# Layer two's search with its bounds made earlier and its probes in halves; three low parts of the first weights on GpSimd, loads held until the first rows land

## The chip, the cores and the metric

The program runs on one core of one Trainium2 chip. The metric is the device time of one execution in microseconds. Engines are named as the profile names them: PE is TensorE (PEld its weight loads), DVE is VectorE, ACT is ScalarE, POOL is GpSimd, SP is SyncE, which issues the plain transfers.

## The reference

Attention, then two mixture-of-experts layers over 1792 tokens of 768 numbers, 8 experts of 768 x 1024 x 768, all in float32. The change is about layer two, where every expert takes exactly 224 tokens and the pairs of token and expert are served in order of their logit.

```python
def _moe2_ref(x, w_gate, w1, w2):
    N, D = x.shape
    E = w_gate.shape[1]
    cap = N // E
    logits = x @ w_gate
    order = np.argsort(-logits.flatten())
    assigned = -np.ones(N, dtype=np.int64)
    counts = np.zeros(E, dtype=np.int64)
    for idx in order:
        tok, e = (int(idx) // E, int(idx) % E)
        if assigned[tok] >= 0 or counts[e] >= cap:
            continue
        assigned[tok] = e
        counts[e] += 1
    out = np.zeros((N, D), dtype=np.float32)
    for e in range(E):
        mask = assigned == e
        h = np.maximum(x[mask] @ w1[e], 0.0)
        out[mask] = h @ w2[e]
    return out
```

## The kernel before

The program computes attention, layer one, and layer two one behind the other; each engine runs its instructions in program order, and there is no scheduler: the order is that of the code. Float32 products are made as three matmuls of a high and a low part each (`w1h xh`, `w1l xh`, `w1h xl`): ScalarE writes the high part as a rounded copy (line 857), VectorE subtracts it from the raw weights for the low part (line 858). A raw block of `w1` is 128 x 1024, 512 KB, and there are six of them, `k` = 0 to 5, for an expert.

Layer two does not sort. It takes the experts in the order in which they fill up, and for each one searches the threshold of the logit at which it is full. All tokens' logits stand in `L` (128 x 14 x 8), the best open one of each token in `t_mm` (128 x 14), its expert as a one-hot in `t_oh`. `search(p)` runs four rounds (`RN`). A round compares `t_mm` with 40 thresholds `thr` (`srch_89`) in one VectorE instruction of 128 x 560, the **probe** (`probe`, line 696, writes `t_g`); counts by 14 small matmuls (line 739); takes the largest excess over the capacity (line 740); makes a flag (`t_ok`, line 744); counts the flags by one matmul (line 752); and writes 40 new thresholds (line 755). After the last round it assigns the tokens (`t_asg`), counts them per expert (`tally`, `t_rab`, line 640 the sum over partitions), and `assign(p)` turns the assignment into a list of 224 row numbers (`idx`). The first bounds of the search come from the smallest and the largest entry of `L` (lines 519 to 533), with two transposes on TensorE (line 524) in the tail of layer one, whose last gate logits run between them (`tail0` to `tail3`, lines 240 to 257).

The search of the first expert to be served (p = 0) runs alone, from 579 to 595 in the trace; dummy groups of matmuls (`warm(n)`, lines 504, 541, 610) stand between its steps on TensorE. Then comes the **head** of layer two. SyncE issues the first weights, GpSimd the gather of the first rows (`gather`, 2 x 112 rows, line 865). The second expert's search is a generator that the head steps through with `go(1)`: its pieces stand in program order between dummy groups, the splitting of the weights (`split`), the transposes of the rows (`take`, which makes `xh` and `xl`, lines 892 to 896), and the first up matmuls (`up4`, line 914). `up4` does the first four of the eight column blocks, `k` by `k`, as the weights come; after it `up(4)` to `up(7)` (line 907) and the rest of the layer run as one stream of matmuls. The head of before in the code:

```python
        for k in range(KD):
            if k:
                go(1)
            if k + 2 < KD:
                split(0, k + 2)
            up4(k, 0, 2)
            if k in (2, 3):
                go(1)
            up4(k, 2, 4)
```

Eight raw buffers (`raw_90` to `raw_97`) take the weights. Before the loads of k = 3 to 7 GpSimd writes one element into each of these buffers (line 941), in its queue behind the gather's issue; so these loads go out when the gather is issued. A buffer is loaded again when both its high and its low part are made.

Of the kernel before, what the change touches and what calls it, by code (L numbers as in the profile page):

```python
# [127 lines left out]
def moe1(tc, w1, w2, wg, xs, y2, l2, ident, before, iob, cr, gt, g0, raw, early, iok, L, srch):  # L128
    nc = tc.nc
    with ExitStack() as c:  # L130
# [380 lines left out]
        d, hp, rh, oi, tk = xg[:, :128], xg[:, 128:256], xg[:, 256:256 + NB * E], xg[:, 512:512 + NB], xg[:, 640:641]  # L511
# [4 lines left out]
        V.scalar_tensor_tensor(hp, d, -float(NB), hp, op0=OP.is_gt, op1=OP.mult)  # L516
        V.tensor_tensor_reduce(d, d, hp, scale=-1.0, scalar=0.0, op0=OP.mult, op1=OP.add, accum_out=tk)
        V.tensor_scalar(oi, iok[:, :NB], tk, None, op0=OP.is_equal)
# [9 lines left out]
        V.tensor_reduce(gmn, pU[0][:, :128], axis=AX.X, op=OP.min)  # L528
        V.tensor_reduce(gmx, pU[0][:, 128:256], axis=AX.X, op=OP.max)
        V.tensor_sub(step, gmx, gmn)  # L530
        V.scalar_tensor_tensor(gmn, step, -0.25, gmn, op0=OP.mult, op1=OP.add)
        V.tensor_scalar(step, step, 1.5 / TH, None, op0=OP.mult)
        V.tensor_scalar(thr, iok[:, :TH], step, gmn, op0=OP.mult, op1=OP.add)
# [3 lines left out]
                     l2c[:, None, :].to_broadcast([128, NB, E]))  # L537
        nc.tensor.matmul(pU[1][:, :NB * E], hp, rh, start=True, stop=True)
# [5 lines left out]
def moe2(tc, w1, w2, y2, out, ident, before, ones, io8, iok, iob16, L, srch, raw, force):  # L544
# [7 lines left out]
    with ExitStack() as c:  # L552
# [141 lines left out]
        def probe():  # L694

            V.tensor_tensor(T["g"][:, :, :TH], T["mm"][:, :, None].to_broadcast([128, PT, TH]),
                            thr[:, None, :].to_broadcast([128, PT, TH]), op=OP.is_ge)

        def search(p):

            if p:
                best()
                V.tensor_tensor(T["oh"], T["lm"], T["m"][:, :, None].to_broadcast([128, PT, E]), op=OP.is_equal)
            else:
                V.tensor_reduce(T["mm"], L, axis=AX.X, op=OP.max)
                probe()
                V.tensor_tensor(T["oh"], L, T["mm"][:, :, None].to_broadcast([128, PT, E]), op=OP.is_equal)
            if p == E - 1:
# [23 lines left out]
            for r in range(RN):  # L732
# [24 lines left out]
                if r < RN - 1:  # L757
                    probe()
# [7 lines left out]
            if p == 0:  # L766
# [3 lines left out]
            V.scalar_tensor_tensor(apen, T["asg"], -BIG, apen, op0=OP.mult, op1=OP.add)  # L770
            V.scalar_tensor_tensor(T["full"], cap, 0.0, left, op0=OP.is_equal, op1=OP.mult)
            V.tensor_tensor_reduce(T["d"], t, T["capm"], scale=1.0, scalar=-3.0e38, op0=OP.subtract,
                                   op1=OP.max, accum_out=T["fl"][:, 0:1])

        def assign(p):

            V.tensor_reduce(T["em"], T["full"], axis=AX.X, op=OP.min)
            V.tensor_scalar(T["fl"][:, :2], T["fl"][:, :2], 0.0, None, op0=OP.not_equal)
            V.tensor_scalar(T["ei"], T["em"], 8.0, 7.0, op0=OP.add, op1=OP.min)
            EV[p] = nc.values_load(T["ei"][0:1, 0:1], engines=[SP], min_val=0, max_val=E - 1)  # L780
            V.tensor_scalar(T["mem"], own, T["em"], None, op0=OP.is_equal)
# [3 lines left out]
            V.scalar_tensor_tensor(bad, T["fl"][:, 0:1], T["fl"][:, 1:2], bad, op0=OP.mult, op1=OP.add)  # L785
            V.tensor_tensor_scan(T["cum"], T["mem"], T["mem"], 0.0, op0=OP.add, op1=OP.bypass)
            V.scalar_tensor_tensor(left, left, T["em"], left, op0=OP.not_equal, op1=OP.mult)
# [18 lines left out]
            for i in range(PT):  # L806
                nc.tensor.matmul(t[:16, :NA], T["b"][:, i], T["a"][:, i], start=(i == 0), stop=(i == PT - 1))
# [639 lines left out]
```

## Time and profile before

| | |
|---|---|
| median of 3 runs | 922.82 us (922.36 to 924.37) |
| the profiled execution | 920.12 us |
| its span on the core | 918.2 us |
| mean granted TensorE clock | 0.991 |
| PE busy | 867.1 us (94%) |
| DVE busy | 594.1 us (65%) |
| ACT busy | 475.1 us (52%) |
| POOL busy | 188.2 us (20%) |

The profiled execution is one further run; 1.9 us of it lie outside the span. Shares over the whole span average stages with different limits: the head of layer two is 13 us of it, and is to be read by itself.

### The profile page before, as it was taken

To read this page: it belongs to the slowest core of one execution; us is meant where nothing else is said; L and a number is where in the kernel's file an instruction comes from. 1 tells how busy PE (TensorE), PEld (TensorE's weight loads), DVE (VectorE), ACT (ScalarE), POOL (GpSimd) and SP (SyncE) were. 2 spreads that over 40 slices of the span, in tenths; PEclk is the share of its full clock that TensorE was granted. 3 is DMA by queue.
4 is the path that set the end of the run, shared out by engine and by line. 5 is a ranking of instruction groups with operands and counts; after the bars stand their busy time and mean duration, and the time that the engine had idled before them with its cause. 6 is when DMAs were issued, how large, how long until landed. Compare 5 with 4: busy or idle time off the path is not lost. (4 is left out here: it accounts for less than half of the span.)

```text
span 918.2 us, 18445 instructions
## 1 busy us (share of the span) xinstructions
PE 867.1 (94%) x6387; PEld 721.9 (79%) x6387; DVE 594.1 (65%) x1741; ACT 475.1 (52%) x1029; POOL 188.2 (20%) x249
## 2 busy tenths in 40 slices
PE   7999999987999998798999999889999999999997
PEld 5666666646788886676888888368989999999997
DVE  7779898877464526738611141798888798875641
ACT  8777777655454527648622242134545344545541
POOL 6644444041111111112111110101101011011001
PEclk9999999998999999999999999999999999999999
DMA  6553537148374616838721110177666575666810
GB/s 177 135 154 102 142 102 225 54 151 296 130 273 157 222 38 228 330 118 309 282 73 53 38 48 33 67 257 245 198 213 200 156 236 177 223 196 193 261 59 30
DMA packets 73921, 151.07 MB, mean 165 GB/s; under 512 B 30513, under 2 KB 38737, under 8 KB 73746
## 3 DMA queue, kind: packets, MB, share of 16 engines
q1 hardware_dynamic: 67602, 123.33, 41.2%
q0 software_dynamic: 6144, 25.72, 8.6%
q8 instruction: 72, 1.18, 0.5%
q14 instruction: 103, 0.84, 0.3%
HBM read 130.34 MB, written 18.67 MB: 162 GB/s over the span
## 5 line engine op out<-in xcount | busy, mean ns | idle before, releaser
L213 PE MATMUL pU<-w1h,xx 128*128 128x512 f32 x336 | 117.9, 408 | 3.7 <-ACT yr L236 1.6
L907 PE MATMUL w<-xh,w1h 128*128 128x224 f32 x360 | 102.2, 284 | 0.8 <-ACTq L995 0.8
L907 PE MATMUL w<-xh,w1l 128*128 128x224 f32 x360 | 99.0, 275 | 0.4 <-DVEq L995 0.4
L1163 ACT ACTIVATE p<-p,nm 112x112 f32<-112x112 f32 (+2 forms) x192 | 98.8, 517 | 0.7 <-DVE nm L1155 0.7
L907 PE MATMUL w<-xl,w1h 128*128 128x224 f32 x360 | 99.0, 275 | 0.0
L1155 DVE CUSTOM_DVE_ANT_0 p<-s,msk 112x112 f32<-112x112 f32 (+2 forms) x192 | 75.9, 444 | 22.5 <-PE s L1152 22.3
L930 PE MATMUL w<-w2h,hh 128*112 128x384 f32 x256 | 89.8, 351 | 0.0
L930 PE MATMUL w<-w2h,hl 128*112 128x384 f32 x256 | 86.5, 338 | 0.0
L930 PE MATMUL w<-w2l,hh 128*112 128x384 f32 x256 | 86.0, 336 | 0.0
L213 PEld LDWEIGHTS pU<-w1h,xx 128*128 128x128 f32 x336 | 62.8, 188 | 21.1 <-issue 2.6
L907 PEld LDWEIGHTS w<-xh,w1h 128*128 128x128 f32 x360 | 69.0, 192 | 1.5 <-ACTq L995 1.0
L907 PEld LDWEIGHTS w<-xh,w1l 128*128 128x128 f32 x360 | 69.1, 192 | 0.6 <-DVEq L995 0.6
L181 DVE TENSOR_TENSOR w2l<-raw,w2h 128x768 fp32r<-128x768 f32 x64 | 58.2, 956 | 17.1 <-ACT w2h L179 14.4
L907 PEld LDWEIGHTS w<-xl,w1h 128*128 128x128 f32 x360 | 69.1, 192 | 0.1
L231 PE MATMUL pY<-w2h,hh 128*128 128x384 f32 x224 | 60.6, 353 | 7.6 <-ACT w1h L179 4.7
L858 DVE TENSOR_TENSOR w2l<-raw,w2h 128x768 fp32r<-128x768 f32 x64 | 60.9, 951 | 8.6 <-ACT w2h L857 8.3
L213 PE MATMUL pU<-w1l,xx 128*128 128x512 f32 x168 | 65.8, 395 | 0.6 <-DVE w1l L460 0.6
L858 DVE TENSOR_TENSOR w1l<-raw,w1h 128x1024 fp32r<-128x1024 f32 x48 | 58.0, 1220 | 9.6 <-ACT w1h L857 9.3
L919 ACT ACTIVATE hh<-w 128x224 fp32r<-128x224 f32 x64 | 22.8, 357 | 79.0 <-PE w L907 56.1
L181 DVE TENSOR_TENSOR w1l<-raw,w1h 128x1024 fp32r<-128x1024 f32 x42 | 49.6, 1218 | 21.8 <-ACT w1h L179 21.8
L869 POOL DMA_INDIRECT out_dram<-yo,idx x15 | 15.2, 1011 | 218.2 <-ACT yo L933 181.8
L231 PE MATMUL pY<-w2l,hh 128*128 128x384 f32 x224 | 58.4, 342 | 0.0
(332 smaller groups left out, 2080.7 us busy)
## 6 DMA issues: line engine op xcount, KB each, us to landing
raw<-in_moe_w_dram SPq DMA_DIRECT2D x96, 512.0 KB
raw<-in_moe_w_dram SPq DMA_DIRECT2D x128, 384.0 KB
vt<-in_v_dram SPq DMA_DIRECT2D x48, 112.0 KB
qr<-in_q_dram SPq DMA_DIRECT2D x23, 224.0 KB
kr<-in_k_dram SPq DMA_DIRECT2D x23, 224.0 KB
xs<-xr SPq DMA_DIRECT2D x4, 1120.0 KB
xs<-xr SPq DMA_DIRECT2D x4, 238.0 KB
y<-yr SPq DMA_DIRECT2D x1, 384.0 KB
```

Of the source, the lines that this page charges most:

```text
L181: nc.vector.tensor_sub(l, r, h.bitcast(F32))
L213: nc.tensor.matmul(pU[half], a[:, k], w[:, k, cs], start=(m == 0), stop=(m == 17))
L231: nc.tensor.matmul(pY[g][:, :384], a[:, k], w[:, k, g * 384:(g + 1) * 384], start=(k == 0 and t == 0), stop=(k == KF - 1 and t == 2))
L858: V.tensor_sub(l, r, h.bitcast(F32))
L869: nc.gpsimd.indirect_dma_start(out=out, out_offset=bass.IndirectOffsetOnAxis(ap=idx[p % 3][:, g:g + 1], axis=0), in_=yo[:, g], in_offset=None)
L907: nc.tensor.matmul(u, w[:, k, fs], x[:, k], start=(k == 0 and n == 0), stop=(k == KD - 1 and n == 2))
L919: A.activation(hh[:, f], u, AF.Relu)
L930: nc.tensor.matmul(y, a[:, f, g * G2:(g + 1) * G2], w[:, f, hf * 384:(hf + 1) * 384], start=(f == 0 and n == 0), stop=(f == KF - 1 and n = ...
L1155: nc.vector.tensor_tensor_reduce(P[u, h][:, o:o + w], s[h][:, :w], msk[:, S - w:], scale=-0.125, scalar=3.0e38, op0=OP.add, op1=OP.min, ac ...
L1163: nc.scalar.activation(p, p, AF.Exp, bias=RS[u, "m"][:, h, i:i + 1], scale=-1.0, accum_out=RS[u][:, h, i:i + 1])
```

## The change

In the tail of layer one, the smallest and the largest entry of `L` are VectorE's first instructions, into a slice of their own (`mn2`), and the two transposes stand ahead of the gate's on TensorE; two groups of two dummy matmuls are left out, and `thr` is written later. In the first search the probe is issued as two instructions of 7 x 40, each a wait of its own for the matmuls, and `t_oh` is made ahead of it. The tally is merged with the comparison; the checks (`bad`, `t_fl`, `left`, `apen`) are put into `rest()`, which runs behind the running count (`cum`) of `assign`, or follow the matmuls of line 807. GpSimd issues a gather by a list of zeros before the search. The highs of k = 0 to 2 stand together ahead on ScalarE, followed by a copy of one element of the gathered rows into `raw[3]`, for which the loads of k = 3 and on wait on SyncE. The lows of k = 2, 3 and 5 are made by GpSimd. `up4` takes the products in two parts.

```diff
+        V.tensor_reduce(mn2[:, 0:1], L, axis=AX.XY, op=OP.min)
+        V.tensor_reduce(mn2[:, 1:2], L, axis=AX.XY, op=OP.max)
+        for n in range(2):
+            nc.tensor.transpose(pU[0][:, n * 128:n * 128 + 128], mn2[:, n:n + 1].to_broadcast([128, 128]), ident)
         V.tensor_copy(tk, sin)
...
-        V.tensor_reduce(d[:, 0:1], L, axis=AX.XY, op=OP.min)
-        V.tensor_reduce(d[:, 1:2], L, axis=AX.XY, op=OP.max)
-        tail1()
-        warm(2)
-        for n in range(2):
-            nc.tensor.transpose(pU[0][:, n * 128:n * 128 + 128], d[:, n:n + 1].to_broadcast([128, 128]), ident)
...
+        def probe(parts=1):
+
+            for i in range(parts):
+                s = slice(i * PT // parts, (i + 1) * PT // parts)
+                n = s.stop - s.start
+                V.tensor_tensor(T["g"][:, s, :TH], T["mm"][:, s, None].to_broadcast([128, n, TH]),
+                                thr[:, None, :].to_broadcast([128, n, TH]), op=OP.is_ge)
...
-                    probe()
+                    probe(1 if p else 2)
+            V.scalar_tensor_tensor(T["ao"], T["mm"][:, :, None].to_broadcast([128, PT, E]), thr[:, 0:1], T["oh"],
+                                   op0=OP.is_ge, op1=OP.mult)
+            with nc.allow_low_precision("small whole numbers"):
+                V.tensor_reduce(T["rab"], T["ao"].rearrange("p i e -> p e i"), axis=AX.X, op=OP.add)
             V.tensor_scalar(T["asg"], T["mm"], thr[:, 0:1], None, op0=OP.is_ge)
-            V.tensor_scalar(T["fl"][:, 2:3], T["fl"][:, 2:3], float(PT), None, op0=OP.not_equal)
-            tally()
-            V.tensor_add(bad, bad, T["fl"][:, 2:3])
             owned()
...
             V.tensor_tensor_scan(T["cum"], T["mem"], T["mem"], 0.0, op0=OP.add, op1=OP.bypass)
-            V.scalar_tensor_tensor(left, left, T["em"], left, op0=OP.not_equal, op1=OP.mult)
+            while late:
+                late.pop()()
...
             V.tensor_scalar(T["ev"], t[:16, :NA], float(N), None, op0=OP.min)
-            if p == 0:
-                warm(2)
...
-        def split(p, k):
+        def split(p, k, part=(True, True), on=V):
...
-            A.activation(h, r, AF.Copy)
-            V.tensor_sub(l, r, h.bitcast(F32))
+            if part[0]:
+                A.activation(h, r, AF.Copy)
+            if not part[1]:
+                return
+            on.tensor_sub(l, r, h.bitcast(F32))
...
-        def up4(k, f0, f1):
-            for f in range(f0, f1):
-                if k == 0:
+        def up4(k, part):
+            p = [(w1h, xh), (w1h, xl), (w1l, xh)]
+            if k < 2:
+                p = [p[0], p[2], p[1]]
+            for f in range(4):
+                if k == 0 and part == 0:
                     U[f] = wt()[:, :CAP]
-                for n, (w, x) in enumerate(((w1h, xh), (w1l, xh), (w1h, xl))):
-                    nc.tensor.matmul(U[f], w[:, k, f * 128:(f + 1) * 128], x[:, k], start=(k == 0 and n == 0),
-                                     stop=(k == KD - 1 and n == 2))
+                for w, x in p[2:] if part else p[:2]:
+                    nc.tensor.matmul(U[f], w[:, k, f * 128:(f + 1) * 128], x[:, k],
+                                     start=(k == 0 and (w, x) == (w1h, xh)), stop=(k == KD - 1 and part == 1))
...
         reset()
+        nc.gpsimd.memset(idx[0], 0)
+        gather(0, 1)
         finish(0)
         for k in range(3):
             load(0, k)
         gather(0)
+        for k in range(3):
+            split(0, k, (True, False))
+        A.activation(raw[3][:1, :1], xg[:1, 1, :1], AF.Copy)
         for k in range(3, NR):
-            nc.gpsimd.memset(raw[k][:1, :1], 0.0)
             load(0, k)
...
-        split(0, 0)
+        split(0, 0, (False, True))
...
-        split(0, 1)
+        split(0, 1, (False, True))
+        split(0, 2, (False, True), nc.gpsimd)
...
-            if k + 2 < KD:
-                split(0, k + 2)
-            up4(k, 0, 2)
+            if 3 <= k + 3 < KD:
+                split(0, k + 3, on=V if k == 1 else nc.gpsimd)
+            up4(k, 0)
             if k in (2, 3):
                 go(1)
-            up4(k, 2, 4)
+            up4(k, 1)
```

On GpSimd, the head of layer two stood like this before: the first expert's gather, five one-element writes, and the next expert's gather.

```order
L865 DMA xg<-y_103,idx_23704 112x768 x2
L941 MEMSET raw_93 1x1
L941 MEMSET raw_94 1x1
L941 MEMSET raw_95 1x1
L941 MEMSET raw_96 1x1
L941 MEMSET raw_97 1x1
L865 DMA xg<-y_103,idx_23705 112x768 x2
```

And now (the first of the three gathers is the one by zeros):

```order
L951 MEMSET idx_23702 112x2
L877 DMA xg<-y_103,idx_23702 112x768 x3
L870 TENSOR_TENSOR w1l<-raw_92,w1h 128x1024
L870 TENSOR_TENSOR w1l<-raw_93,w1h 128x1024
L870 TENSOR_TENSOR w1l<-raw_95,w1h 128x1024
L877 DMA xg<-y_103,idx_23703 112x768 x2
```

Three subtractions took the place of the five writes, each behind the high part of its block.

On VectorE, from the low parts of the rows (`xl`) to the probe of the second search's last round, before:

```order
L896 TENSOR_TENSOR xl<-w,xh 128x448 x3
L858 TENSOR_TENSOR w1l<-raw_92,w1h 128x1024
L740 ISA t_d,t_mx<-gp,t_capm 40x8
L740 ISA t_mx 40x1
L744 TENSOR_SCALAR t_ok<-t_mx 40x1
L748 ISA t_ao,t_fl<-t_oh 128x112
L748 ISA t_fl 128x1
L858 TENSOR_TENSOR w1l<-raw_93,w1h 128x1024
L755 SCALAR_TENSOR_TENSOR srch_89<-gp,steps,t_base 128x40
L696 TENSOR_TENSOR t_g<-t_mm,srch_89 128x14x40
```

And now:

```order
L908 TENSOR_TENSOR xl<-w,xh 128x448 x3
L743 ISA t_d,t_mx<-gp,t_capm 40x8
L743 ISA t_mx 40x1
L747 TENSOR_SCALAR t_ok<-t_mx 40x1
L751 ISA t_ao,t_fl<-t_oh 128x112
L751 ISA t_fl 128x1
L870 TENSOR_TENSOR w1l<-raw_94,w1h 128x1024
L758 SCALAR_TENSOR_TENSOR srch_89<-gp,steps,t_base 128x40
L697 TENSOR_TENSOR t_g<-t_mm,srch_89 128x14x40
```

One subtraction is left in this piece, that of k = 4; behind the probe another (`raw_94` before) and one later (`raw_95`) are gone too.

On TensorE, in the tail of layer one, from the branch on, before (`pU_3390` are the two transposes of the bounds, `pB` and `pA` the gate's):

```order
L444 UNCONDITIONAL_BRANCH
L240 MATMUL pB_3388<-ident,yr 128x128 x4
L240 MATMUL pB_3389<-ident,yr 128x128 x2
L504 LDWEIGHTS before
L504 MATMUL pU_3391<-iob,before 128x512
L504 LDWEIGHTS before
L504 MATMUL pU_3391<-iob,before 128x512
L524 MATMUL pU_3390<-ident,xg 128x128 x2
L250 MATMUL pA_3387<-hb,wg_101 32x128 x4
```

And now:

```order
L444 UNCONDITIONAL_BRANCH
L515 MATMUL pU_3390<-ident,xg 128x128 x2
L240 MATMUL pB_3388<-ident,yr 128x128 x4
L240 MATMUL pB_3389<-ident,yr 128x128 x2
L250 MATMUL pA_3387<-hb,wg_101 32x128 x4
```

The bounds' transposes moved from between the gate's two steps to ahead of both, and the dummy pair between them is gone.

## Rows read from the trace of the kernel before

**Rows 1.** Windows by stage: us, busy (instructions) by engine, clock, DMA share.

```profile
605.20:618.00 12.80, 10.86 (x104) 9.69 (x104) 12.01 (x46) 5.35 (x9) 0.00 (x0) 1.00 0.77 277
618.00:630.00 12.00, 12.00 (x107) 11.69 (x106) 10.56 (x23) 7.64 (x15) 2.51 (x6) 1.00 0.67 202
650.00:912.00 262.00, 258.93 (x2086) 246.65 (x2085) 187.33 (x533) 117.61 (x193) 27.61 (x27) 1.00 0.57 183
```

**Rows 2.** TensorE's waits from 605.2 to 625: total, times, longest us.

```profile
PE gp L739 <- DVE t_g L696: 0.6, 1, 0.6
...
PE gp L752 <- DVE t_ok L744: 0.4, 1, 0.4
```

**Rows 3.** Timeline where the search is set up: start, duration us.

```profile
575.73 0.60 ACT L241 ACTIVATE hb<-pB 128x512 f32<-128x512 f32 x1 [0.42 <-PE pB L240]
...
576.71 0.43 PE L250 MATMUL pA<-hb,wg 128*32 128x128 f32 x8
```

**Rows 4.** Timeline, a later round of the first search.

```profile
583.28 0.51 PE L739 MATMUL gp<-t_oh,t_g 128*40 128x8 bf16 x14 [0.16 <-DVE t_g L696]
```

**Rows 5.** Timeline, end of the first assignment on TensorE.

```profile
594.05 0.60 PE L610 MATMUL w<-iob,before 128*128 128x512 bf16 x2
...
594.59 0.21 PE L813 MATMUL gp<-t_ev,sel 16*112 16x15 f16 x1
```

**Rows 6.** Timeline of the head, first layer-two expert.

```profile
597.45 1.06 ACT L857 ACTIVATE w1h<-raw 128x1024 fp32r<-128x1024 f32 x1 [0.69 <-DMA raw<-in_moe_w_dram]
...
600.33 0.74 DVE L696 TENSOR_TENSOR t_g<-t_mm,srch 128x560 bf16<-128x560 f32 x1
...
601.40 1.22 DVE L858 TENSOR_TENSOR w1l<-raw,w1h 128x1024 fp32r<-128x1024 f32 x1
...
605.26 0.37 PE L914 MATMUL w<-xh,w1h 128*128 128x224 f32 x1
...
605.95 3.91 ACT L857 ACTIVATE w1h<-raw 128x1024 fp32r<-128x1024 f32 x4
...
610.07 0.74 DVE L696 TENSOR_TENSOR t_g<-t_mm,srch 128x560 bf16<-128x560 f32 x1
...
610.87 0.51 PE L739 MATMUL gp<-t_oh,t_g 128*40 128x8 bf16 x14 [0.64 <-DVE t_g L696]
...
618.12 0.27 PE L907 MATMUL w<-xh,w1h 128*128 128x224 f32 x1
```

**Rows 7.** Groups by form, GpSimd: count, busy us, mean ns.

```profile
L1138 POOL TENSOR_TENSOR kl<-kr,kh 128x448 fp32r<-128x448 f32 x23 | 26.5, 1152 | 1.8
```

**Rows 8.** Timeline, GpSimd and VectorE together, and line 1283 (min/median/max).

```profile
71.68 1.16 POOL L1138 TENSOR_TENSOR kl<-kr,kh 128x448 fp32r<-128x448 f32 x1
...
71.76 1.13 DVE L1283 TENSOR_TENSOR eq<-lg,mx 112x32 f32<-112x32 f32 x1
...
L1283 DVE TENSOR_TENSOR eq<-lg,mx x4: 181/598/1132, 71.8 to 189.8; 112x32 f32<-112x32 f32 x4
```

**Rows 9.** Timeline of GpSimd while VectorE subtracts.

```profile
198.04 1.19 POOL L478 TENSOR_TENSOR hb<-jn,early 128x112 f32<-128x112 f32 x1
...
201.22 0.37 POOL L483 TENSOR_TENSOR hb<-gt 128x112 f32<-128x112 f32 x1
```

**Rows 10.** The gather's queue in 600:600.5 and 601:601.5, share of 16 engines.

```profile
q0 software_dynamic: 27, 0.14, 84.8%
...
q0 software_dynamic: 10, 0.03, 17.5%
```

**Rows 11.** TensorE's waits from 180 to 230, as rows 2.

```profile
PE pA L265 <- DMA xg<-xs,nx: 3.4, 1, 3.4
```

**Rows 12.** Windows of 1 us around an idle TensorE; columns as rows 1.

```profile
216.00:217.00 1.00, 0.00 (x0) 0.00 (x0) 0.41 (x1) 0.00 (x0) 0.00 (x0) 0.50 1.01 408
...
221.00:222.00 1.00, 1.00 (x5) 1.00 (x4) 1.00 (x2) 0.00 (x0) 0.00 (x0) 0.50 0.95 370
...
223.00:224.00 1.00, 1.00 (x7) 1.00 (x6) 0.00 (x0) 0.00 (x0) 0.00 (x0) 1.00 0.84 291
```

More of the change, by code (lines that the diff above doesn't have):

```diff
@@ L516, in moe1 @@
         V.scalar_tensor_tensor(hp, d, -float(NB), hp, op0=OP.is_gt, op1=OP.mult)
+        V.tensor_reduce(gmn, pU[0][:, :128], axis=AX.X, op=OP.min)
+        V.tensor_reduce(gmx, pU[0][:, 128:256], axis=AX.X, op=OP.max)
+        tail1()
         V.tensor_tensor_reduce(d, d, hp, scale=-1.0, scalar=0.0, op0=OP.mult, op1=OP.add, accum_out=tk)
+        V.tensor_sub(step, gmx, gmn)
         V.tensor_scalar(oi, iok[:, :NB], tk, None, op0=OP.is_equal)
[L519 to L524 removed]
+        V.scalar_tensor_tensor(gmn, step, -0.25, gmn, op0=OP.mult, op1=OP.add)
+        V.tensor_scalar(step, step, 1.5 / TH, None, op0=OP.mult)
         tail2()
         warm(2)
[L528 to L533, printed above, removed]
         tail3(False)
@@ L692, in best @@
             V.tensor_add(T["mm"], T["m"], apen)
-        def probe():
-            V.tensor_tensor(T["g"][:, :, :TH], T["mm"][:, :, None].to_broadcast([128, PT, TH]),
-                            thr[:, None, :].to_broadcast([128, PT, TH]), op=OP.is_ge)
+        def probe(parts=1):
[4 more added lines that the diff above has]
+                                thr[:, None, :].to_broadcast([128, n, TH]), op=OP.is_ge)
+        late = []
         def search(p):
@@ L705, in search @@
                 V.tensor_reduce(T["mm"], L, axis=AX.X, op=OP.max)
-                probe()
                 V.tensor_tensor(T["oh"], L, T["mm"][:, :, None].to_broadcast([128, PT, E]), op=OP.is_equal)
+                probe(2)
             if p == E - 1:
@@ L769, in search, with rest @@
             V.tensor_sub(cap, cap, t)
-            V.scalar_tensor_tensor(apen, T["asg"], -BIG, apen, op0=OP.mult, op1=OP.add)
             V.scalar_tensor_tensor(T["full"], cap, 0.0, left, op0=OP.is_equal, op1=OP.mult)
-            V.tensor_tensor_reduce(T["d"], t, T["capm"], scale=1.0, scalar=-3.0e38, op0=OP.subtract,
-                                   op1=OP.max, accum_out=T["fl"][:, 0:1])
+            def rest():
+                V.tensor_tensor_reduce(T["d"], t, T["capm"], scale=1.0, scalar=-3.0e38, op0=OP.subtract,
+                                       op1=OP.max, accum_out=T["fl"][:, 0:1])
+                V.scalar_tensor_tensor(apen, T["asg"], -BIG, apen, op0=OP.mult, op1=OP.add)
+                V.tensor_scalar(T["fl"][:, 2:3], T["fl"][:, 2:3], float(PT), None, op0=OP.not_equal)
+                V.tensor_add(bad, bad, T["fl"][:, 2:3])
+            late.append(rest)
         def assign(p):
             V.tensor_reduce(T["em"], T["full"], axis=AX.X, op=OP.min)
-            V.tensor_scalar(T["fl"][:, :2], T["fl"][:, :2], 0.0, None, op0=OP.not_equal)
+            V.tensor_scalar(T["mem"], own, T["em"], None, op0=OP.is_equal)
             V.tensor_scalar(T["ei"], T["em"], 8.0, 7.0, op0=OP.add, op1=OP.min)
             EV[p] = nc.values_load(T["ei"][0:1, 0:1], engines=[SP], min_val=0, max_val=E - 1)
-            V.tensor_scalar(T["mem"], own, T["em"], None, op0=OP.is_equal)
             with nc.allow_low_precision("small whole numbers"):
@@ L807, in assign @@
                 nc.tensor.matmul(t[:16, :NA], T["b"][:, i], T["a"][:, i], start=(i == 0), stop=(i == PT - 1))
+            V.tensor_scalar(T["fl"][:, :2], T["fl"][:, :2], 0.0, None, op0=OP.not_equal)
+            V.scalar_tensor_tensor(left, left, T["em"], left, op0=OP.not_equal, op1=OP.mult)
+            V.scalar_tensor_tensor(bad, T["fl"][:, 0:1], T["fl"][:, 1:2], bad, op0=OP.mult, op1=OP.add)
             V.tensor_scalar(T["ev"], t[:16, :NA], float(N), None, op0=OP.min)
-            if p == 0:
-                warm(2)
             yield YY[9]
@@ L861, in split, with gather @@
                 flush()
-        def gather(p):
-            for g in range(2):
+        def gather(p, n=2):
+            for g in range(n):
                 nc.gpsimd.indirect_dma_start(out=xg[:, g], out_offset=None, in_=y2,
```

5 lines of the change are left out of this document (2 added, 3 removed).

## The prediction

> **What bounds the kernel now.** I read the table of windows by stage first [rows 1]. From 618 on TensorE works almost without a gap: 12.00 of 12 us to 630, and 258.93 of 262 from 650 to 912. What stands there is matmul work, which the change leaves as it is. So the end of the kernel moves with the moment at which `up(4)` starts, 618.12 in the trace [rows 6], and only what lies ahead of that is to be costed. There, in the stage from 605.2 to 618, VectorE is busy 12.01 of 12.80 us, TensorE 10.86 and GpSimd not at all [rows 1]. Then I read TensorE's waits of that stage: the longest are for a probe (`t_g`, 0.6) and for a flag of the search (`t_ok`, 0.4) [rows 2]. VectorE makes both, in program order, between two-operand subtractions of 1.22 us (`w1l`) [rows 6]: the second expert's search is threaded through this stage as a chain of probe, 14 small matmuls, max, flag, one matmul, new threshold. Last I followed the timeline from 574 to 618 instruction by instruction at the places that the change touches [rows 3 to 6].
>
> **The change, part by part.**
>
> *Bounds of the search off the chain.* The gate's matmuls start at 576.71, behind the two transposes of the bounds, while their operand `hb`, written from 575.73 for 0.60, is there at 576.33 [rows 3]. With the transposes ahead of everything: −0.3 (0 to −0.45, since the threshold row also leaves the way of the gate's last reduce on VectorE). The two pairs of dummy matmuls dropped here I take to cost no clock, since TensorE has real work on both sides of each; were it to fall, rows 12 give the price (below).
>
> *Probes in halves, first expert.* A probe takes 0.74 us [rows 6] and its 14 matmuls 0.51 [rows 4], one after the other. In halves, seven matmuls (0.25) run under the second half; a second VectorE instruction has a start of its own, for which I take 0.08 (bounds 0, fully overlapped, and 0.25, which eats the gain). So −0.17 in each of three later rounds, −0.5; in the first round other short VectorE work ends last, −0.1. Bounds 0 and −0.75.
>
> *Tally, flags, dummy matmuls.* The merged tally shortens VectorE's chain by one short instruction, but the deferred flags come back ahead of the column of the assignment: I take 0. The dropped pair of dummy matmuls ran from 594.05 for 0.60, and the selection behind it starts only at 594.59 [rows 5], though its operand is made by some 0.2 earlier: −0.2 (0 to −0.25).
>
> Sum of the search: −1.1 (0 to −1.45).
>
> *Loads held until the rows land.* ScalarE's one-element copy waits for the second gather. The gather's queue fills 84.8% of the engines from 600 to 600.5 and 17.5% from 601 to 601.5 [rows 10], so the rows are nearly all there at 601, and a microsecond earlier with the shorter search, without the loads beside them. The held loads (k = 3 to 7) then go out at about 600.9 at the latest. Queued behind the copy on ScalarE are the `xh` and behind these the highs, which start at 605.95 [rows 6]. So the first held load has 5.0 us for its 512 KB; at the 277 GB/s of this stage [rows 1] a load takes 1.9, and three take 5.7 against highs that stand at 605.95, 606.9 and 607.9. Cost 0, covered by `xh`; without the cover each late us is a us on the highs of k = 3 to 5, some 1.7 at most.
>
> *The dummy gather* ahead of the search is GpSimd's alone, long before the real ones: 0.
>
> *Three low parts on GpSimd.* No row has this operation 1024 wide. The nearest is the subtraction of 448 columns, 1152 ns [rows 7]; by columns that is 2.63 us, less a fixed part, so I take 2.55 (bounds 2.4 and 2.65). VectorE is relieved of three times 1.22. Do the two engines work side by side? The trace says no: at 71.68 GpSimd subtracts for 1.16, VectorE's compare starts at 71.76 and shows 1.13, ending with it, where the same instruction takes 181 ns at best [rows 8]. The other way round, a GpSimd operation of 112 columns shows 1.19 beside VectorE's subtractions, and the next of its kind 0.37 when VectorE is idle [rows 9]. So I let each low part on GpSimd stop VectorE's probes and subtractions (two inputs in SBUF) until it ends, up to its 2.55.
>
> The Trainium skill has a price for the operation: "GPSIMD Engine Reference", section 3.1, gives 4497 ns for 2048 columns, as an estimate 2.25 for 1024; with it the three parts would take 0.9 us less in all, and the sum would be some 0.7 lower. The row of 448 columns is of this program, so its 2.55 stands. The Trainium skill's "SBUF — State Buffer", "Who interferes with whom", speaks against this part of the change: a VectorE instruction with two SBUF inputs and a GpSimd instruction that reads SBUF exclude one another, and the later one waits for the whole of the other. The rows of 71.7 agree (1.13 beside 1.16).
>
> Now the order of events. (1) The high of k=1 starts as its load lands, 597.45, and takes 1.06 [rows 6]. With k=2's load a little over one us behind, and all of it 1.1 earlier, the high of k=2 is done at about 598.7, and low k=2 holds GpSimd from there to 601.3. The probe that now starts at 600.33 would start at 599.2; it waits until 601.3 and ends at 602.0. The `w1l` of k=1 (1.22, at 601.40) [rows 6] ran under ten dummy matmuls; now it stands behind the probe and ahead of the max of its round, about 0.7 later in all than before: first up matmul at 605.26 + 0.7 = 605.96. So low k=2 costs 1.8, and the search's gain is spent. (2) The highs start at 605.95 + 0.7 and take 3.91 for four [rows 6], so that of k=3 is there at 607.7, that of k=5 at 609.6. Low k=3 runs from 607.8 to 610.4; in it VectorE stops at the square of `t_oh` that follows the flag. GpSimd then stands in line with k=5 while VectorE has its one short instruction, and takes the turn: 610.6 to 613.1. Behind it VectorE has `w1l` of k=4 (1.22, to 614.3), the new threshold (0.3) and the probe (0.74): the last round's matmuls at 615.3, 9.35 after the first up matmul. Before it was 610.87 − 605.26 = 5.61 [rows 6]. +3.7. (3) From there to `up(4)` it was 618.12 − 610.87 = 7.25, with two more `w1l` on VectorE, which are gone. What is left is TensorE's own: 40 up matmuls at 0.112 (107 in 12.00) [rows 1] and the round's small ones, 1.1: 5.6. −1.6. So +2.8 at `up(4)`.
>
> (4) TensorE then stands still from about 610.2 to 615.3. Elsewhere in this trace it waited 3.4 us for a transfer [rows 11]; the granted clock stood at 0.50 (of 2.4 GHz, so 1.2) at the end of that, still so with TensorE fully busy from 221 to 222, and was back at 1.00 from 223 [rows 12]. So I expect some five us at half clock here, in which an up matmul takes nearly twice its 0.112. A dozen of them stand on the path while the search's own chain covers the others: +1.0 (0 to +2).
>
> **Sum.** The profiled execution took 920.12: −1.1 + 1.8 + 3.7 − 1.6 + 1.0 = +3.8, 923.9. The median of the three runs shown lies 2.70 above that execution, so I forecast 926.6.
>
> **The rivals.**
>
> (a) *GpSimd works beside VectorE* (other side). VectorE loses 3.7 us of work in its fullest stage, both waits of [rows 2] go, and the search's 1.1 arrives in full. The stage is then TensorE's: 72 up matmuls, 8.1, small ones 1.6, and 0.7 of the chain's hops from 604.2 on: `up(4)` at 614.6, −3.4: 919.4. For it: VectorE bounds the stage while GpSimd idles. Against: 71.7. It decides if a probe beside a GpSimd subtraction keeps its 0.74.
>
> (b) *They exclude one another, but VectorE gets in between.* If low k=5 comes only after the last probe, (2) loses its 2.55 and most of the rest is given back in (3); the idle stretch is too short for the clock: 0 to +0.5, 922.8 to 923.3. For it: only 0.8 us lies between k=5's high (609.6) and the turn (610.4).
>
> (c) *Held loads late.* With the rows two us after my 600.9, the highs of k = 3 to 5 set the stage: +1.7 on (a), 921.1; on the forecast it disappears in the waits.
>
> (d) *The search gains nothing*, because VectorE's short instructions set its steps: +0.6 on the forecast (927.2), 1.1 on (a) (920.5).
>
> **How the numbers follow.** The forecast, with (d) on it and its own range 924.8 to 928.6 (clock 0 or +2, low parts 2.4 or 2.65): 0.52. (b): 0.18. (a): 0.22. (c) or (d) on (a): 0.08. A measurement of this kernel tells about 0.2% (1.85 us) from no change: faster is below 921.0, slower above 924.7. Faster: (a) 0.22 and 0.03 of (c), (d), 0.25. Same: 0.15 of (b), 0.05 of (c), (d), 0.20. Slower: 0.52 and 0.03 of (b), 0.55. The range has to reach (a) and most of the forecast's: 919.3 to 928.5.
>
> **What would show it.** Right: `w1l` on GpSimd of 2.4 to 2.7 us; a probe or subtraction on VectorE recorded at 1.5 us or more beside one; a TensorE wait for the last round's probe of 3 us or more with a granted clock near 0.5 behind it; `up(4)` at about 621; in the first search, small matmuls that begin before the second half of the probe ends. Wrong: probes of 0.74 at most and `up(4)` before 616 is (a); `up(4)` near 618 and no wait over 1.5 is (b); a ScalarE wait for `raw` of k=3 behind the `xh` is (c).

## The result: 929.46 us, 0.84% slower, with the half clock twice in the head

The changed kernel takes 929.46 us as a median of seven executions (928.07 to 934.31), the kernel before 922.57 beside it; the ratio is 1.0084, 95% interval 1.0066 to 1.0101. The direction was the one forecast, the size was not: 926.6 was expected, and 929.46 lies above the top of the range, 928.5. The profiled execution took 928.47 with a span of 926.5, 8.3 more than before. One slow execution of 1206.12 us, of the kernel before with eight more dummy matmuls, is left out of that version's ratio below.

The timeline of the changed kernel through the head (start, duration; the rows of before stand in [rows 6]):

```profile
600.18 0.74 DVE L697 TENSOR_TENSOR t_g<-t_mm,srch 128x560 bf16<-128x560 f32 x1
...
601.01 2.34 POOL L870 TENSOR_TENSOR w1l<-raw,w1h 128x1024 fp32r<-128x1024 f32 x1 [3.52 <-ACT w1h L867]
601.03 2.36 DVE L738 TENSOR_SCALAR t_base<-iok,steps,t_col 128x40 f32<-128x40 f32 x1
...
605.84 2.45 PE L904 MATMUL w<-ident,xg 112*128 112x112 f32 x12
...
607.96 0.54 PE L929 MATMUL w<-xh,w1h 128*128 128x224 f32 x1
...
609.89 4.73 POOL L870 TENSOR_TENSOR w1l<-raw,w1h 128x1024 fp32r<-128x1024 f32 x2 [6.54 <-ACT w1h L867]
...
610.68 1.73 DVE L751 CUSTOM_DVE_ANT_0 t_ao<-t_oh 128x112 f32<-128x112 bf16 x1
...
612.34 3.37 DVE L870 TENSOR_TENSOR w1l<-raw,w1h 128x1024 fp32r<-128x1024 f32 x1
...
616.71 0.63 PE L742 MATMUL gp<-t_oh,t_g 128*40 128x8 bf16 x14 [3.62 <-DVE t_g L697]
...
624.71 0.27 PE L919 MATMUL w<-xh,w1h 128*128 128x224 f32 x1
```

GpSimd's low part of k=2 (2.34) came at 601.01, behind the probe and not ahead of it as forecast, and caught VectorE at `t_base`, an instruction on 40 columns that takes 0.30 elsewhere and shows 2.36 here. The two others ran as one block from 609.89 to 614.6: the square of `t_oh` shows 1.73 instead of 0.26, and the subtraction of k=4 3.37 instead of 1.22. The first two end within 0.15 us of the low part beside them, the third only after the whole of the last one. First up matmul 607.96, last round 616.71, `up(4)` 624.71, where it was 605.26, 610.87 and 618.12.

TensorE's waits from 592 to 630 show the same from the other side (before: [rows 2]), one of 3.6 us and one of 1.8:

```profile
PE gp L742 <- DVE t_g L697: 4.6, 2, 3.6
PE gp L755 <- DVE t_ok L747: 2.3, 2, 1.8
```

The windows of 1 us (columns as in [rows 1]) add what was mis-sized. The granted clock falls from 1.00 (2.4 GHz) to 0.50 (1.2 GHz) twice: once behind the wait of 1.8 us (TensorE 0.15 busy from 604 to 605), and once towards the end of that of 3.6 (idle from 614 to 615), from where half clock lasts past 622:

```profile
604.00:605.00 1.00, 0.15 (x2) 0.14 (x3) 0.93 (x5) 0.00 (x0) 0.00 (x0) 1.00 0.96 381
606.00:607.00 1.00, 1.00 (x8) 1.00 (x7) 0.47 (x3) 0.17 (x1) 0.00 (x0) 0.50 1.45 225
...
614.00:615.00 1.00, 0.00 (x0) 0.00 (x0) 1.00 (x1) 0.00 (x0) 0.62 (x1) 1.00 0.84 295
617.00:618.00 1.00, 1.00 (x14) 0.98 (x12) 0.38 (x4) 0.00 (x0) 0.00 (x0) 0.50 0.84 304
621.00:622.00 1.00, 1.00 (x6) 1.00 (x6) 0.91 (x9) 0.00 (x0) 0.00 (x0) 0.50 0.00 0
623.00:624.00 1.00, 1.00 (x11) 0.98 (x11) 0.44 (x3) 0.00 (x0) 0.00 (x0) 1.00 0.00 0
```

At 606 the twelve transposes of the rows take 2.45 at half clock; before, at full clock, they took 1.32. A third piece lies far from the change. From `up(4)` to the end of the span there are 301.8 us, where it was 300.1. TensorE stops once, behind the branch near the end, in the middle of a stream of matmuls whose operands are long there:

```profile
889.43 0.27 PE L919 MATMUL w<-xh,w1l 128*128 128x224 f32 x1
891.03 0.37 PE L919 MATMUL w<-xl,w1h 128*128 128x224 f32 x1 [1.33 <-DVE w2l L870]
```

The wait of 1.33 is put down to a VectorE subtraction, but the matmul that ends it needs nothing of it; the experiments say more on this below.

Times are best compared from VectorE's first instruction behind the branch ahead of the search, since that point itself moves by some tenths to three us from execution to execution. For before and after it, and the gate's first transposes:

```profile
574.31 0.15 DVE L512 CAST xg<-sin 128x1 f32<-128x1 int32 x1 [3.66 <-PEq L441]
...
574.98 0.93 PE L240 MATMUL pB<-ident,yr 128*128 128x128 f32 x6 [0.80 <-ACT yr L236]
```

```profile
574.63 0.27 DVE L512 TENSOR_REDUCE xg<-L 128x1 f32<-128x112 f32 x1 [3.63 <-PEq L441]
...
575.66 0.40 PE L515 MATMUL pU<-ident,xg 128*128 128x128 f32 x2 [1.16 <-ACT yr L236]
...
575.90 0.82 PE L240 MATMUL pB<-ident,yr 128*128 128x128 f32 x6
```

`up(4)` then lies 43.81 us behind the branch before the change, and 50.08 after it: +6.27. That measure is used below ("behind the branch").

### The profile page after: what moved, and what is told of

Its sections match the earlier page's. It is cut to its first block, busy times and chain, and to the rows that moved or that the text cites. A ratio compares the mean times of both kernels' runs of the same rounds, so it can differ in the third digit from the quotient of the medians.

```text
span 926.5 us, 18425 instructions
## 1 busy us (share of the span) xinstructions
PE 869.6 (94%) x6383; PEld 725.1 (78%) x6383; DVE 599.4 (65%) x1742; ACT 475.6 (51%) x1030; POOL 198.8 (21%) x249
## 5 line engine op out<-in xcount | busy, mean ns | idle before, releaser
L867 ACT ACTIVATE w1h<-raw 128x1024 fp32r<-128x1024 f32 x48 | 48.3, 1051 | 20.1 <-DMA raw<-in_moe_w_dram 19.6
```

Source lines behind the costliest of these rows:

```text
L867: A.activation(h, r, AF.Copy)
```

## The experiments

Diffs are against the changed kernel where nothing else is said. Ratios are to the kernel before on the same chip; its own medians in the three groups were 921.92, 923.67 and 923.44.

### The three low parts back on VectorE

```diff
-        split(0, 2, (False, True), nc.gpsimd)
...
-            if 3 <= k + 3 < KD:
-                split(0, k + 3, on=V if k == 1 else nc.gpsimd)
+            if k + 2 < KD:
+                split(0, k + 2, (k > 0, True))
```

> The changed kernel with the low parts of k = 2, 3 and 5 back on VectorE, in the places they had before; all else of the change stays. If GpSimd's subtractions are the cost by stopping VectorE: no VectorE instruction of the head over 1.3 us, no wait of TensorE over 1.0 for a probe, granted clock 1.00 from 605 to 627, up(4) at 617 to 618.2, time 921.5 to 923.5. If instead the held loads or the earlier gather cost the time: ScalarE waits for raw of k = 3 or 4, up(4) stays beyond 621, time 926 or more.

Measured: 922.34, ratio 1.0006 (0.9989 to 1.0023). The loss is gone, and with it every stretched VectorE instruction. But the profile has half clock in the head here too, earlier, from 600 to 604: ten dummy matmuls take 4.02 instead of 2.33, and `up(4)` is at 44.60 behind the branch; with that stretch at full clock it is at 42.94 (the run with fillers below).

```profile
574.97 0.27 DVE L512 TENSOR_REDUCE xg<-L 128x1 f32<-128x112 f32 x1 [3.79 <-PEq L441]
...
600.13 4.02 PE L608 MATMUL w<-iob,before 128*128 128x512 bf16 x10
...
619.57 0.27 PE L919 MATMUL w<-xh,w1h 128*128 128x224 f32 x1
```

### The kernel before with the three low parts on GpSimd

Against the kernel before:

```diff
-        def split(p, k):
+        def split(p, k, on=V):
...
-            V.tensor_sub(l, r, h.bitcast(F32))
+            on.tensor_sub(l, r, h.bitcast(F32))
...
-                split(0, k + 2)
+                split(0, k + 2, V if k == 2 else nc.gpsimd)
```

> The kernel before with one edit: the low parts of k = 2, 3 and 5 on GpSimd. Exclusion: three GpSimd subtractions of 2.3 to 2.4 us one behind the other from about 607 to 614, VectorE's subtraction of k = 4 or the probe recorded over 2 us, a TensorE wait of 2 to 4 us before the last round, up(4) at 621 to 623, time 926 to 928.5. Rival, that search and held loads make the loss: 922 to 924.

Measured: 929.58, ratio 1.0075 (1.0055 to 1.0095). So this one part alone makes a loss as large as the whole change; `up(4)` is at 51.13 behind the branch against 43.81. Three subtractions in a row, 7.55 us, and the probe beside them shows 2.60 instead of 0.74:

```profile
602.21 4.02 PE L610 MATMUL w<-iob,before 128*128 128x512 bf16 x10
...
611.06 7.55 POOL L858 TENSOR_TENSOR w1l<-raw,w1h 128x1024 fp32r<-128x1024 f32 x3 [10.06 <-ACT w1h L857]
...
613.79 2.60 DVE L696 TENSOR_TENSOR t_g<-t_mm,srch 128x560 bf16<-128x560 f32 x1
```

It is 1.1 us above what was expected, since the clock fell twice here as well. The first time was ahead of all low parts: the dummy matmuls took 4.02 in a stretch of instructions that is the same as in the kernel before, whose profile has 2.33 there. So part of this run's loss, some 1.7 us at the first up matmul (32.62 behind the branch against 30.95), is not made by the low parts.

### Each low part in four pieces

```diff
-            on.tensor_sub(l, r, h.bitcast(F32))
+            n = 1 if on is V else 4
+            w = l.shape[-1] // n
+            for i in range(n):
+                c = slice(i * w, (i + 1) * w)
+                on.tensor_sub(l[:, c], r[:, c], h[:, c].bitcast(F32))
```

> The changed kernel with each GpSimd low part issued as four subtractions of 256 columns. If the engines exclude one another for a whole instruction and take turns: each piece 0.6 to 0.7 us, VectorE's instruction at the first low stretched to under 1.0 instead of 2.36, the subtraction of k = 4 under 2.0 instead of 3.37, probe of the last round at 614 to 615 instead of 615.9, first up matmul before 606.8, time 924 to 927. If they share the port evenly by bandwidth, the length of the instruction plays no part: same stretches, 929 to 930.

Measured: 928.43, ratio 1.0062 (1.0040 to 1.0084). At the second and third low part the stretches are as the exclusion for a whole instruction has it: the square 0.53 instead of 1.73, the subtraction of k=4 1.75 instead of 3.37, and the last round's matmuls 6.31 after the first up matmul instead of 8.75. At the first no VectorE instruction was caught: the subtraction of k=1 was already running, and GpSimd's first piece took 1.21 instead of 0.72. The time is not as expected: it was out by 1.4 us. `up(4)` comes at 47.20 behind the branch, 2.9 before the changed kernel's, although half clock stood at 601 to 604 and at 615 to 621. But from `up(4)` to the end it takes 304.4 us, where the changed kernel took 301.8: half clock comes with the late stop (1.32 here), from 888 to past 894. So shorter turns did shorten the wait, and most of the gain was lost again some 270 us later.

```profile
609.30 7.06 POOL L874 TENSOR_TENSOR w1l<-raw,w1h 128x256 fp32r<-128x256 f32 x8 [3.40 <-ACT w1h L867]
...
610.32 0.53 DVE L751 CUSTOM_DVE_ANT_0 t_ao<-t_oh 128x112 f32<-128x112 bf16 x1
...
610.78 1.75 DVE L874 TENSOR_TENSOR w1l<-raw,w1h 128x1024 fp32r<-128x1024 f32 x1
```

```profile
890.00:891.00 1.00, 1.00 (x6) 1.00 (x6) 0.00 (x0) 0.00 (x0) 0.00 (x0) 0.50 0.00 0
```

### Dummy matmuls in the two long waits

```diff
+        def fill(n):
+            t = small(128)
+            for _ in range(n):
+                nc.tensor.matmul(t, before, iob16[:, None, :].to_broadcast([128, 1, 128]), start=True, stop=True)
...
-        warm(2)
+        warm(9)
         go(1)
         warm(3)
...
+            if k == 2:
+                fill(54)
             if k in (2, 3):
                 go(1)
```

> The changed kernel with dummy matmuls in the two long waits of TensorE (seven more groups of 512 columns ahead of the flag of the second round, 54 of 128 columns ahead of the last round's small matmuls). If the half clock follows from TensorE standing idle: granted clock 1.00 from 605 to 627, the rows' transposes 1.3 instead of 2.45, first up matmul near 606.9, last round to up(4) near 6 instead of 8.0, time 926 to 927.5. If the clock falls for another reason, or the fillers come in the way: 929 to 931.

Measured: 924.28, ratio 1.0022 (1.0007 to 1.0038): 1.7 us below what was expected, by work that computes nothing (the stop of 1.3 us behind the late branch is absent here too). The clock stays at 1.00 throughout (the windows below; at 606 and 617 it was 0.50), and the last round to `up(4)` takes 5.73 (616.55 to 622.28) instead of 8.00. `up(4)` is at 46.66 behind the branch. VectorE's stretches are close to those of the changed kernel (2.31, of `t_col` in place of `t_base`, 1.48 and 3.38, against 2.36, 1.73 and 3.37). So 46.66 is where the exclusion without the clock puts `up(4)`, and 50.08 − 46.66 = 3.42 is the clock's, by one profile of each.

```profile
575.62 0.27 DVE L512 TENSOR_REDUCE xg<-L 128x1 f32<-128x112 f32 x1 [3.50 <-PEq L441]
...
607.90 0.37 PE L929 MATMUL w<-xh,w1h 128*128 128x224 f32 x1
...
616.55 0.51 PE L742 MATMUL gp<-t_oh,t_g 128*40 128x8 bf16 x14 [0.35 <-DVE t_g L697]
...
622.28 0.27 PE L919 MATMUL w<-xh,w1h 128*128 128x224 f32 x1
```

```profile
606.00:607.00 1.00, 1.00 (x7) 0.68 (x8) 0.87 (x3) 0.00 (x0) 0.00 (x0) 1.00 0.88 287
...
617.00:618.00 1.00, 1.00 (x10) 0.87 (x8) 0.47 (x4) 0.00 (x0) 0.00 (x0) 1.00 0.81 310
```

### Eight dummy matmuls in the head's short waits

```diff
-                warm(6)
+                warm(8)
...
-        warm(7)
+        warm(11)
         go(1)
-        warm(2)
+        warm(4)
```

On the version with the low parts on VectorE (the diff against it):

> All low parts on VectorE, the rest of the change kept, and eight more dummy matmuls in TensorE's short waits between 593 and 600 (two, four and two). If the clock's fall at 600 to 604 in the profile of the run before it follows from these waits: granted clock 1.00 through the head, the ten dummy matmuls in 2.3 instead of 4.0, up(4) some 42.9 us after VectorE's first instruction behind the branch (43.8 in the kernel before), time 919 to 921, with a smaller spread. If the fall has another cause: clock 0.5 again in the head, 922 to 923.5.

Measured: 922.00, ratio 0.9987 (0.9975 to 0.9999), above what was expected as a time. In the profile the step is right: the ten matmuls take 2.33, `up(4)` is at 42.94 behind the branch.

```profile
577.53 0.27 DVE L512 TENSOR_REDUCE xg<-L 128x1 f32<-128x112 f32 x1 [3.73 <-PEq L441]
...
602.70 2.33 PE L608 MATMUL w<-iob,before 128*128 128x512 bf16 x10
...
607.89 0.37 PE L929 MATMUL w<-xh,w1h 128*128 128x224 f32 x1
...
613.27 0.51 PE L742 MATMUL gp<-t_oh,t_g 128*40 128x8 bf16 x14
...
620.47 0.27 PE L919 MATMUL w<-xh,w1h 128*128 128x224 f32 x1
```

And on the kernel before:

> The kernel before with the same eight dummy matmuls. If some executions of the kernel before lose time to a clock fall in the head, as the spread of its times (919.4 to 924.8) suggests: median 920 to 921, spread smaller, clock 1.00 in the head. If not: 922 and the same spread. The difference to the run with the search's changes beside it is what these are worth: 0.9 expected.

Measured: 923.25, ratio 0.9997 (0.9983 to 1.0012), no difference. So the guess that these waits cost the kernel before time in many of its executions is not borne out. The first up matmul and `up(4)` are where they were without the fillers (30.95 and 43.80 behind the branch, in the profile). Between the two runs lie 0.86 us in the profile and 1.25 in the medians (where the two intervals overlap): that is the search, with what else of the change is left. Of the 0.86, 0.51 is there when the first expert's list is made (20.24 behind the branch against 20.75); the other 0.35 comes in the head.

### The bounds behind the gate's transposes

Against the version with fillers:

```diff
-        for n in range(2):
-            nc.tensor.transpose(pU[0][:, n * 128:n * 128 + 128], mn2[:, n:n + 1].to_broadcast([128, 128]), ident)
         V.tensor_copy(tk, sin)
...
-        V.tensor_reduce(gmn, pU[0][:, :128], axis=AX.X, op=OP.min)
-        V.tensor_reduce(gmx, pU[0][:, 128:256], axis=AX.X, op=OP.max)
         tail1()
+        for n in range(2):
+            nc.tensor.transpose(pU[0][:, n * 128:n * 128 + 128], mn2[:, n:n + 1].to_broadcast([128, 128]), ident)
         V.tensor_tensor_reduce(d, d, hp, scale=-1.0, scalar=0.0, op0=OP.mult, op1=OP.add, accum_out=tk)
+        V.tensor_reduce(gmn, pU[0][:, :128], axis=AX.X, op=OP.min)
+        V.tensor_reduce(gmx, pU[0][:, 128:256], axis=AX.X, op=OP.max)
```

> The fillers' version with the two transposes of the bounds, and the two reduces of VectorE that read them, put behind the gate's six transposes. In the changed kernel the bounds' transposes start at 575.66, when ScalarE's copies end, and the gate's behind them. If that order cost what the earlier bounds were to bring: the gate's transposes begin 0.6 us earlier against the branch, up(4) 0.3 to 0.5 earlier, time 0.3 to 0.5 lower than the fillers' version. Rival: the chain of VectorE sets the start of the search, no difference.

Measured: 920.50, ratio 0.9971 (0.9956 to 0.9985): the lowest ratio of all versions, below 1 by more than its interval. The gate's transposes start 0.67 behind the branch, as before the change, instead of 1.27; `up(4)` is at 42.40.

```profile
575.46 0.27 DVE L512 TENSOR_REDUCE xg<-L 128x1 f32<-128x112 f32 x1 [3.75 <-PEq L441]
...
576.13 0.93 PE L240 MATMUL pB<-ident,yr 128*128 128x128 f32 x6 [0.80 <-ACT yr L236]
...
617.86 0.28 PE L919 MATMUL w<-xh,w1h 128*128 128x224 f32 x1
```

### Two low parts on GpSimd, k = 3 and 5

```diff
-        split(0, 2, (False, True), nc.gpsimd)
...
+            if k == 0:
+                split(0, 2, (False, True))
             if 3 <= k + 3 < KD:
```

> The changed kernel with k = 2 back on VectorE, k = 3 and 5 still on GpSimd. Exclusion: the head up to the first up matmul as with all three on VectorE (31.5 to 32.1 us behind the branch, clock aside), then 4.7 us in which VectorE's probe and subtraction stand, TensorE waiting 2.5 to 4 us before the last round and half clock behind it: 926 to 928.5. Rival, that the low part of k = 2 made most of the loss: 922.5 to 924.

Measured: 930.45, ratio 1.0086 (1.0057 to 1.0115); `up(4)` at 48.92. By time it is as bad as all three, and by `up(4)` 1.2 us better, so the low part of k=2 is not the main one. The high of k=5 came late here, since ScalarE waited for the held blocks (0.33 for k=3, 1.47 for k=4, 0.37 for k=5); so VectorE's subtraction of k=4 came between the two low parts, and the second one caught the probe itself (2.65). TensorE waited 4.0 us, and half clock lasted from 613 to 623. Half clock comes with the late stop here too, and from `up(4)` to the end it takes 304.7 us.

```profile
607.60 2.75 POOL L870 TENSOR_TENSOR w1l<-raw,w1h 128x1024 fp32r<-128x1024 f32 x1 [9.76 <-ACT w1h L867]
...
608.29 2.19 DVE L751 CUSTOM_DVE_ANT_0 t_ao<-t_oh 128x112 f32<-128x112 bf16 x1
...
611.54 2.34 POOL L870 TENSOR_TENSOR w1l<-raw,w1h 128x1024 fp32r<-128x1024 f32 x1 [1.20 <-ACT w1h L867]
...
611.83 2.65 DVE L697 TENSOR_TENSOR t_g<-t_mm,srch 128x560 bf16<-128x560 f32 x1
```

### Three kinds of operation on GpSimd

Against the fastest version, that with the bounds behind the gate's transposes:

```diff
         gather(0)
+        R = T["R"].rearrange("p a b -> p (a b)")
+        nc.gpsimd.memset(R, 0.0)
+        nc.gpsimd.tensor_scalar(R, R, 1.0, None, op0=OP.add)
+        nc.gpsimd.tensor_sub(R[:, :1024], R[:, :1024], R[:, 512:1536])
```

> The fastest version so far (low parts on VectorE, fillers, bounds behind the gate's transposes), with three extra operations on GpSimd behind the first gather, on a tile that nothing else reads here: a memset of 1792 columns, an add of one to them (one input in SBUF), a subtraction of 1024 (two inputs). If only GpSimd operations that read SBUF stop VectorE's two-operand instructions: VectorE's subtraction of k = 0 (1.22) or the probe unchanged under the memset, and stretched (probe over 1.0, subtraction over 1.5, or t_base over 0.6) under the add and the subtraction. If any work of GpSimd stops VectorE: stretched under the memset too. If only two-input operations do: the add stretches nothing. The time of the run tells little, 920 to 924.

Measured: 926.17, one execution. All three stretch something. Beside the memset it is a VectorE operation of five columns with its scalars in SBUF (1.67 instead of 0.23); no two-operand instruction met the memset, so that half of the question stays open. Beside the add it is `t_base` (4.62 by its record), beside the subtraction the product of `t_oh` (2.36 instead of 0.26). But the add did not hold VectorE to its end: the subtraction of k=0, with two inputs, starts at 602.96, 3.2 us after `t_base` and within the add, and takes 1.39, not the 1.5 or more that was expected.

```profile
597.83 1.67 DVE L734 TENSOR_SCALAR steps<-fine,srch 128x5 f32<-128x5 f32 x1
597.86 1.61 POOL L958 MEMSET t_R<- 128x1792 f32 x1
...
599.55 4.75 POOL L959 TENSOR_SCALAR t_R<-t_R 128x1792 f32<-128x1792 f32 x1
599.73 4.62 DVE L738 TENSOR_SCALAR t_base<-iok,steps,t_col 128x40 f32<-128x40 f32 x1
...
602.96 1.39 DVE L870 TENSOR_TENSOR w1l<-raw,w1h 128x1024 fp32r<-128x1024 f32 x1
...
604.39 2.34 POOL L960 TENSOR_TENSOR t_R<-t_R 128x1024 f32<-128x1024 f32 x1
...
604.50 2.36 DVE L622 TENSOR_TENSOR t_ao<-t_oh,io 128x112 f32<-128x112 bf16 x1
```

### Loads not held, and no dummy gather

The fastest version with the one-element writes of before in place of ScalarE's copy, and the same version without the gather by zeros:

```diff
-        A.activation(raw[3][:1, :1], xg[:1, 1, :1], AF.Copy)
         for k in range(3, NR):
+            nc.gpsimd.memset(raw[k][:1, :1], 0.0)
             load(0, k)
```

> The same fastest version with the loads of k = 3 and on released by GpSimd's one-element writes behind the gather's issue, as in the kernel before, instead of by the rows' landing. If holding the loads costs nothing: no difference beyond 0.1 per cent, up(4) within 0.4 us. If the held loads are late for k = 5 (ScalarE waited 0.5 us for it with the low parts on VectorE): 0.3 to 0.6 faster. If they were in the gather's way: rows land a microsecond later and the transposes start later, 0.5 to 1 slower.

Measured: 921.12, ratio 0.9983 (0.9969 to 0.9996), against 0.9971 with the loads held; `up(4)` at 42.53 behind the branch.

```diff
-        nc.gpsimd.memset(idx[0], 0)
-        gather(0, 1)
```

> The same fastest version without the gather by zeros ahead of the search. The real gather then starts 0.9 instead of 0.3 us after its list is made, as in the kernel before. Forecast's term, that it is worth nothing: no difference beyond 0.1 per cent. Rival, that the rows' landing holds the loads and through them the head: 0.3 to 0.6 slower.

Measured: 920.62, ratio 0.9972 (0.9956 to 0.9988); `up(4)` at 42.28. Both are within 0.15 us of the 42.40 by the profile, and their intervals overlap. Neither edit shows an effect here.

## Why the forecast was wrong, step by step

**What sets the end: right but for one stop.** Where TensorE does not stop behind the late branch, the distance from the branch to `up(4)` tells the runs apart: from `up(4)` to the end it is 300.0 to 300.4 us in all of them. The stop was not foreseen, and the forecast had nothing for it. It stands in the profiles of the changed kernel, of the low parts back on VectorE, in pieces, and of k = 3 and 5 (1.2 to 1.5 each), and in none of the kernel before and its variants, nor of the versions with fillers. At full clock it costs 1.5 to 1.7 us (the first two); where half clock comes with it, 4.3 and 4.6 (the last two). In the versions with dummy matmuls some 280 to 290 us earlier, eight or 61 of them, it is absent. What holds TensorE there stays open.

**Bounds off the chain, −0.3: wrong in sign.** The transposes stand on TensorE ahead of the gate's, and start only 1.03 behind the branch, about when ScalarE's copies of the rows and VectorE's first six instructions end (which of the two holds them stays open); the gate's transposes start 0.60 later, and the gate's matmuls, which were to gain 0.3, 0.16 later (2.56 behind the branch against 2.40). With the bounds behind the gate's transposes these matmuls start at 2.07, the 0.3 that was forecast, and `up(4)` comes 0.54 earlier (42.94 to 42.40).

**Search in sum, −1.1: half of it with the order of the change, all of it with the other.** At the list of the first expert it is −0.51 with the bounds first and −1.06 with the bounds behind (19.69 against 20.75 behind the branch); at `up(4)` 0.86 and 1.40, with what the head adds. The halves gave 0.10 a round, not 0.17: the rounds follow every 2.18 us, before every 2.28. The dropped dummy pair gave the 0.2, and what else was moved there, taken as 0, cost as much: from the last round's small matmuls to the list it is 7.19 us in the changed kernel and 7.21 before.

**Loads held and dummy gather, 0 each: right**, though the rows land at 602.3 and not at 600.9. In the changed kernel ScalarE goes from the `xh` to the highs without a wait: the cover was long enough. The two edits above were tried on the fastest version only.

**Low parts on GpSimd, 2.55 each and exclusive: right in kind, a little too long.** They take 2.34 to 2.41 each, about the lower bound of 2.4. The Trainium skill's "GPSIMD Engine Reference", section 3.1, led to 2.25 as an estimate, nearer than the 2.55 by columns.

**Stops, +1.8, +3.7, −1.6, together +3.9: right.** With the clock kept up, the changed kernel has `up(4)` at 46.66; without low parts on GpSimd at 42.94: +3.7. The parts came out at +1.9 (first up matmul 32.28 against 30.36), +3.3 (8.65 to the last round against 5.38) and −1.5 (5.73 to `up(4)` against 7.20). Only the first stop was of another instruction than named: the low part of k=2 came 2.3 us late, and missed the probe. Its block landed late: the high of k=2 starts at 599.87, 2.35 behind that of k=1, where the forecast had a little over one; and the loads came no earlier with the shorter search (highs of k=0 and 1 at 595.71 and 597.52, before at 595.70 and 597.45).

**(4) Half clock, +1.0 (0 to +2): this is the step that failed.** It measured +3.4. "A dozen of them stand on the path while the search's own chain covers the others" was wrong: half clock lasted over five of the 8.00 us from the last round to `up(4)`, and TensorE worked without a gap there, so nearly every matmul of that stretch counted (8.00 instead of 5.73, 2.3). And the step asked for the clock at one wait only. The wait of 1.8 us ahead of it, which follows from the first stop, brought it down as well (1.05, first up matmul).

In sum, against the kernel before: −0.9 for the search, +3.7 for the stops, +3.4 for the clock, +1.7 from `up(4)` to the end: +7.9 of the 8.3 by which the spans differ (0.3 more lie ahead of the branch). The forecast had −1.1, +3.9, +1.0 and 0. So the clock is the largest miss (+2.4), and the late stop, which no step of the forecast names, the next (+1.7). These are sums of one profiled execution each. The medians lie 6.9 apart and not 8.3; and the other six executions of the changed kernel have a mean granted clock of 0.979 to 0.989, the profiled one 0.991, so they spent more time at half clock than this profile shows. Where, no trace shows.

**The rivals.** (a), side by side, fell: stretched instructions in every run with low parts on GpSimd. (b), VectorE getting in between, did not come in the changed kernel. It came in two variants and helped in neither: with k = 3 and 5 only, the later low part met the probe; in the kernel before with the three low parts, the third stood behind the last probe and stopped `t_col` (2.31 at 616.31), so that TensorE waited 1.8 more for the flag. (c), the loads late, did not come in the changed kernel. In two versions ScalarE did wait for held blocks: 0.5 for k=5 with the low parts on VectorE, where it cost nothing (5.38 from the first up matmul to the last round, as with the loads not held), and up to 1.5 with k = 3 and 5 only. (d), no gain of the search, fell by the profiles of the fillers' pair, and by the ratio of the version with the bounds behind.

## What to carry to other kernels

An engine that idles is not free help: before work is moved to GpSimd, look in the trace for one instruction of VectorE that is longer beside GpSimd than alone, and price a move by the whole duration of each GpSimd instruction on VectorE's chain. If a change opens a TensorE wait of a us or more, read the clock behind it, and count every matmul up to the clock's return twice. A wait that can't be removed may be filled: by the profiles dummy matmuls took back 3.4 us up to `up(4)` here. After a change, look also at stages that it does not touch: a stop that nothing in the change explains cost 1.5 to 4.6 us near the end.

## What the runs showed of the hardware that was not expected

VectorE's operations on few columns with one tensor input and scalars read from SBUF stop beside GpSimd as well (`t_base`, 0.30 to 2.36), and even beside a memset, which reads nothing (0.23 to 1.67). The Trainium skill's "SBUF — State Buffer", "Who interferes with whom", lists this class of instruction among those that can take the shared ports, and sets the stop by two inputs apart, as one against GpSimd's reads only; the row at 597.83 agrees with the first. Of the second, beside a memset, no run here shows anything.

The clock also fell in the head with no wait longer than 1.01 us ahead of it (low parts on VectorE: waits of 0.6, 0.3, 1.0 and 0.6 between 593 and 600), and stayed at 1.00 with these filled. In the kernel before, with 0.4, 0.9 and 0.6, one profile has it at 1.00, and one of the same instructions has it at 0.5. That other profile is of the kernel before with the three low parts, ahead of the first of them. Nor do the low parts on VectorE make the fall: with the same waits it came in the version in pieces too, and not in the changed kernel, nor in the one with fillers in the long waits, nor in that with k = 3 and 5 (1.00 until 605 and later). So behind these short waits either level was met, and one profile does not tell which is the usual one.

A gather by zeros ahead of time shortens the start of the next one: from the list's last instruction to GpSimd's issue it takes 0.28 us with it (594.86 + 0.18 to 595.32) and 0.90 without (596.63 + 0.18 to 597.71, in the run without it). Nothing here waited for that.
